# One mixing of three head groups in the first layer, and the output row in two halves: a two-layer decode kernel

## The chip, the cores and the metric

One core of a Trainium2 chip runs the whole kernel. The metric is the device time of one execution in microseconds; the kernel before takes 644.83 us (median of 3 runs, 644.8 to 645.44).

The engines named below: TensorE (PE; its weight loads are listed as PEld), VectorE (DVE), ScalarE (ACT), GpSimd (POOL) and SyncE (SP), which issues the DMA transfers.

## The reference

Four rows of 512 numbers go through two equal layers. Each layer is attention over a long cache (8 key/value heads, each shared by 4 query heads, 8,192 positions of 128 numbers), and then a gated feed-forward block (512 to 1,792 and back). Both layers read the same cache and the same weights.

```python
def reference(A_x, A_k_cache, A_v_cache, A_wq, A_wo, B_x, B_w_gate, B_w_up, B_w_down):
    def _A_ref(x, k_cache, v_cache, wq, wo):
        ...
        q = (lambda x, *d: x.transpose(*d))((x @ wq).reshape(B, Sq, Hq, Dh), 0, 2, 1, 3)
        ...
        scores = jnp.einsum("bhqd,bhkd->bhqk", q, k) * (Dh ** -0.5)
        p = _softmax(scores, axis=-1)
        o = jnp.einsum("bhqk,bhkd->bhqd", p, v)
        return (lambda x, *d: x.transpose(*d))(o, 0, 2, 1, 3).reshape(B, Sq, Hq * Dh) @ wo

    def _B_ref(x, w_gate, w_up, w_down):
        g = _silu(x @ w_gate)
        u = x @ w_up
        return (g * u) @ w_down

    x = A_x
    x = x + _A_ref(_layernorm(x, axis=-1), A_k_cache, A_v_cache, A_wq, A_wo)
    x = x + _B_ref(_layernorm(x, axis=-1), B_w_gate, B_w_up, B_w_down)
    x = x + _A_ref(_layernorm(x, axis=-1), A_k_cache, A_v_cache, A_wq, A_wo)
    x = x + _B_ref(_layernorm(x, axis=-1), B_w_gate, B_w_up, B_w_down)
    return x
```

## The kernel before

**Units and tiles.** The attention of a layer is cut into 16 units `u`, one for each pair of key/value heads `gp` (4 of them, the "groups") and each of the 4 rows `b`. A unit has one K tile and one V tile of 4 MB each. They lie in four large slots of SBUF, used as a ring, and a fifth slot that holds `wq` first. A K tile is handled in eight pieces: VectorE transposes them in place (`turn`, L567, two pieces at a time in most units), and TensorE multiplies each with the queries (`scores`, L593). Then come the row maximum (L599, L604, L607), the exponential on ScalarE (`exps`, L631 to L644), the transpose of the probabilities (`turn_p`, L659), and the products with V (`values`, L731) in four parts. The result is gathered on VectorE (L779, L783), summed over positions (`combine`, L788) and scaled (L793) into `oT`. Work on the V of one unit runs between the score pieces of the next.

**Two lists set the order.** `blocks` holds the score pieces and the parts of V, each with a cost of 0.9 us. `line` holds small steps, each with a gap in microseconds; after every block `advance` takes the block's cost off the first step's gap and emits the steps that have come due. `flush` emits steps without regard to their gaps, all of them if called without a tag. What the lists decide is the order in each engine's instruction stream, once, while the kernel is built; at run time every engine takes its own stream strictly in that order and waits on semaphores.

**Closing a group.** When the four units of a group are done, `close_group` (L825) sees to the output projection of its 8 heads. For all groups but the last of a layer the heads are first *mixed* (`mix`, L806: 16 small products L815 into PSUM and one copy back, L819), which puts them into the order in which `wo` lies in SBUF; then `rows` (L847) multiplies each head's 4 columns with its 512 columns of `wo` (L850), 8 products a group, adding up in one PSUM bank (`OUTB`). After the last but one group, `upright` (L855) turns the 4 x 512 result back to columns in four steps of a ScalarE copy (L864) and a TensorE transpose (L860), and VectorE adds it to `x` (L804). The last group of a layer goes through `out_proj` instead (L875). In the first layer (`L` = 0) groups 0 and 1 are mixed together after group 1, and their rows are emitted by way of the list `later` at the next end of a unit's values; group 2 is mixed alone after unit 11. In the second layer groups 3, 0 and 1 are mixed together after the third of them.

**The hold.** In the first layer the last two pieces of unit 13's K tile (`half_kept`) are kept for the second layer: `finished` (L536) empties `line` with `flush()` and then `hold` (L522) transposes each piece into two PSUM banks, four in all (L533), among them `OUTB` and `LNB`, which the rows and `upright` use. So all rows and turnings stand ahead of the hold in the streams.

**Transfers.** SP issues a transfer as soon as the slot pieces that it overwrites are freed (`freed`, `pump`), in one fixed order. At the end of the first layer the slot of the W weights takes `w_gate`, `w_up` and `w_down`; the later pieces of `w_down` go where `w_gate` lay and are issued as the first products of the feed-forward block (L1016) release it. K tiles of the second layer follow in the same way.

**The output.** The second layer's feed-forward block puts the output together in PSUM bank `STEP`, in four quarters of 128 columns, quarter `j` on rows 32j to 32j+3. `x_rows` (L889) first puts the residual x there: for each pair `c` of quarters four fp32 products with an identity (L893), each of 64 columns; `x_rows(0)` stands in the middle of `center`, `x_rows(1)` ahead of the last products. Then come 14 x 4 products with `w_down` (L1043), and four copies to SBUF, two on VectorE (L1120), two on ScalarE (L1118), and the output's transfer (L1122). `w_down` arrives in three pieces, for 8, 4 and 2 of the 14 steps.

```python
        def quarter(j):
            return bank(STEP)[j * QB:j * QB + B, 0:P]
```

Of the kernel before, what the change touches and what calls it, by code (L numbers as in the profile page):

```python
# [5 lines left out]
ACTF = mybir.ActivationFunctionType  # L6
# [97 lines left out]
def bass_interleave_layers__gqa_block_cached__swiglu_ffn__decode_kernel(  # L104
# [12 lines left out]
    B, _, D = A_x.shape  # L117
# [5 lines left out]
    P = 128  # L123
# [8 lines left out]
    QB = 32  # L132
# [12 lines left out]
    with ExitStack() as es:  # L145
# [132 lines left out]
        def bank(k):  # L278
            return ps[:, k * BANKF:(k + 1) * BANKF]
# [13 lines left out]
            assert o + b <= BANKF  # L293
            return bank(k)[rows, o + a:o + b], f"pb{k}"

        def quarter(j):
            return bank(STEP)[j * QB:j * QB + B, 0:P]

        sem = lambda name: es.enter_context(nc.semaphore(name))
        engines = {"pe": nc.tensor, "act": nc.scalar, "dve": nc.vector, "pool": nc.gpsimd, "sp": nc.sync}  # L300
# [56 lines left out]
        def spot(L, gp):  # L357
            return groups[L].index(gp)
# [466 lines left out]
        def close_group(L, gp, fill):  # L825
            if gp == groups[L][-1]:
                line.extend([[0.5, None, lambda: mix(L, [gp], fill)], [0.7, None, lambda: out_proj(L, gp, fill)]])
                return
            n = spot(L, gp)
            if n < (1, 2)[L]:  # L830
                return
            gs = groups[L][:n + 1] if n == (1, 2)[L] else [gp]
            line.append([0.5, None, lambda: mix(L, gs, fill)])
            turned_back = upright() if gp == groups[L][-2] else []

            def in_rows():
                while gp not in mixed:
                    line.pop(0)[2]()
                for g in gs:
                    rows(L, g)  # L840
                return turned_back
            if turned_back and not L:
                line.extend([[0.7, None, in_rows]] + turned_back)
            else:
                later.append(in_rows)

        def rows(L, gp):  # L847
            for r in range(H2):
                h, o = gp * H2 + r, spot(L, gp) * H2 + r
                T.op("pe", lambda e: e.matmul(bank(OUTB)[0:B, 0:D], lhsT=oT[:, o, :], rhs=wo_sb[:, h, :],  # L850
                                              start=(gp == groups[L][0] and r == 0),
                                              stop=(gp == groups[L][GP - 2] and r == H2 - 1)),
                     reads=[f"wo{gp}", OT[gp]], writes=[f"pb{OUTB}"], sig=(r == H2 - 1))

        def upright():  # L855
            at, name = bank(LNB)[:, 4 * P - XB:4 * P], f"pb{LNB}"

            def step(kt):
                if kt:
                    T.op("pe", lambda e: e.matmul(at[:, (kt - 1) * B:kt * B], lhsT=row, rhs=identf[0:B, 0:B],  # L860
                                                  is_transpose=True, start=True, stop=True),
                         reads=["row", "ident"], writes=[name])
                if kt < KT:
                    T.op("act", lambda e: e.activation(row, bank(OUTB)[0:B, pick2(kt)], ACTF.Copy),  # L864
                         reads=[f"pb{OUTB}"], writes=["row", "pb"])
                else:
                    add_to_x(at, name)
            return [[0.9, None, lambda kt=kt: step(kt)] for kt in range(KT + 1)]
# [19 lines left out]

        def x_rows(c):  # L889
            for e_ in range(2):  # L890
                for m in range(2):
                    kt, o = 2 * c + e_, m * (P // 2)
                    T.op("pe", lambda e: e.matmul(quarter(2 * c + m)[:, e_::2], lhsT=xT[:, kt * B:(kt + 1) * B],  # L893
                                                  rhs=identf[:, o:o + P // 2], start=(e_ == 0), stop=False),
                         reads=["x", "ident"], writes=[f"pb{STEP}"], sig=(e_ == 1 and m == 1))

        def center(between=lambda: None):
            T.op("dve", lambda e: e.tensor_reduce(xs, xT[:].rearrange("p (k b) -> p b k", b=B), AX.X, ALU.add),
# [98 lines left out]
        def ffn(L):  # L997
# [39 lines left out]
            if L == 1:  # L1037
                x_rows(1)
                for i, (a, b) in enumerate(WDS[1]):
                    for fo in range(a, b):  # L1040
                        for j in range(NA):
                            o = s * SL + O_WD + fo * D + j * P
                            T.op("pe", lambda e: e.matmul(quarter(j), lhsT=hT[:, fo * B:(fo + 1) * B],  # L1043
                                                          rhs=kvf[:, o:o + P], start=False, stop=(fo == FO - 1)),
                                 reads=["hT", f"wd{i}"] + rooms[f"wd{i}"], writes=[f"part{j}"],
                                 sig=(fo == b - 1))
                freed(s, DOWN, NB)
                return
# [63 lines left out]
            ffn(L)  # L1112
        assert issued[0] == len(cmds)

        for j in range(NA):
            to = xio[:, j * P:(j + 1) * P]
            if j % 2:
                T.op("act", lambda e: e.activation(to, quarter(j), ACTF.Copy), reads=[f"part{j}"], writes=[f"y{j}"])  # L1118
            else:
                T.op("dve", lambda e: e.tensor_copy(to, quarter(j)), reads=[f"part{j}"], writes=[f"y{j}"])  # L1120
        T.wait_res("sp", reads=[f"y{j}" for j in range(NA)])
        nc.sync.dma_start(out.rearrange("b s d -> (b s) d"), xio).then_inc(sem_out, 16)  # L1122
        nc.sync.wait_ge(sem_out, 16)

# [27 lines left out]
```

## Time and profile before

| | |
|---|---|
| median of 3 runs | 644.83 us |
| the profiled execution | 645.2 us |
| its span, first to last instruction | 642.9 us, 6,981 instructions |
| TensorE matmul busy | 413.0 us (64%), 2,886 instructions |
| TensorE weight loads | 173.2 us (27%), 2,888 instructions |
| VectorE busy | 424.9 us (66%), 597 instructions |
| ScalarE busy | 50.2 us (8%) |
| moved by DMA | 271.76 MB, mean 423 GB/s |
| mean granted clock of TensorE | 0.834 |
| chain that ended last, by share | DMA 60%, VectorE 19%, TensorE 16% |

The span is what the profile's own clock covers; the time of a run also has what lies around it, 2.3 us here. The granted clock is the share of its full clock that TensorE was given. The *chain of waits* follows the work that ended last back from step to step; the *timeline* lists instructions in order of time, with the idle time of the engine before them and who ended it; *windows* give each engine's busy time in a stretch.

### The profile page before, as it was taken

Reading aid. Unit: us, or ns where it says so; the run is one execution under the profiler, and the core shown is the slowest. Engines: PE = TensorE matmul, PEld = TensorE weight load, DVE = VectorE, ACT = ScalarE, POOL = GpSimd, SP = SyncE. Lnnn points to the kernel's source line nnn. Section 1 sums busy time; section 2 is a strip of 40 time slices with the busy share of each in tenths; the row PEclk is TensorE's granted clock in tenths of the full one; section 3 lists DMA queues with packets and bytes.
Section 4 is the critical chain, followed back from the end, with each engine's and each line's share of the span. In section 5 each row is a group of like instructions: output and inputs, shape, how many; then the busy total and the mean of one; then the engine's idle time right before and its main releaser. Section 6 shows DMA issues by size and latency. Waiting matters only on the chain.

```text
span 642.9 us, 6981 instructions
## 1 busy us (share of the span) xinstructions
PE 413.0 (64%) x2886; PEld 173.2 (27%) x2888; DVE 424.9 (66%) x597; ACT 50.2 (8%) x138; POOL 11.9 (2%) x44
## 2 busy tenths in 40 slices
PE   0583476457755757757866977667655477558766
PEld 0231122122222312222325332222222122223224
DVE  5375467456776656776953888977765567656953
ACT  0100000000000000000010300000000000000110
POOL 0000000000000000000000000000000000000000
PEclk9995886688876898768975899998767987679987
DMA  9999999999999999999999999999999999999996
GB/s 365 451 423 414 436 430 432 433 428 423 436 438 427 426 432 433 433 430 429 428 414 386 416 435 431 433 431 429 434 428 430 435 430 432 424 436 429 431 414 261
DMA packets 16014, 271.76 MB, mean 423 GB/s; under 512 B 1640, under 2 KB 1648, under 8 KB 7536
## 3 DMA queue, kind: packets, MB, share of 16 engines
q1 hardware_dynamic: 15984, 271.33, 99.1%
q8 instruction: 22, 0.36, 0.2%
q14 instruction: 8, 0.07, 0.0%
HBM read 271.32 MB, written 0.00 MB: 422 GB/s over the span
## 4 chain that ended last, share of the span: by engine, by line
DMA 60%; DVE 19%; PE 16%; issue 4%; ACT 0%; SPq 0%; POOL 0%; ACTq 0%; DVEq 0%; POOLq 0%
DMA kvf<-in_A_k_cache_dram 45%; DVE kvf L567 14%; DMA kvf<-in_A_v_cache_dram 11%; PE ps L593 10%; DMA kvf<-in_A_wq_dram 3%; PE ps L731 2%; DVE pb L783 2%; DMA kvf<-in_B_w_down_dram 1%; PE ps L982 1%; PE ps L1016 1%; DVE pT L659 1%; DVE pb L779 0%; DVE ps L533 0%; DVE scr L793 0%; PE ps L875 0%
## 5 line engine op out<-in xcount | busy, mean ns | idle before, releaser
L593 PE MATMUL ps<-kvf,zq 128*128 128x512 bf16 x1024 | 291.8, 431 | 185.6 <-DVE kvf L567 178.6
L567 DVE STREAM_TRANSPOSE kvf<-kvf 128x2048 f32<-128x2048 f32 (+1 forms) x133 | 280.5, 2132 | 125.5 <-DMA kvf<-in_A_k_cache_dram 125.3
L593 PEld LDWEIGHTS ps<-kvf,zq 128*128 128x128 bf16 x1024 | 98.9, 108 | 343.1 <-DVE kvf L567 222.6
L731 PE MATMUL ps<-kvf,pT 128*32 128x512 bf16 x960 | 65.8, 396 | 1.4 <-DVE pT L659 1.4
L641 ACT ACTIVATE pb<-ps,tiny 128x512 bf16<-128x512 f32 x32 | 24.9, 777 | 507.8 <-DVE tiny L639 507.8
L659 DVE STREAM_TRANSPOSE pT<-pb 64x512 bf16<-64x512 bf16 x60 | 41.2, 686 | 3.0 <-ACT pb L641 2.0
L783 DVE SCALAR_TENSOR_TENSOR pb<-ps,tiny,pb 128x128 f32<-128x128 f32 x104 | 36.5, 351 | 5.1 <-PE ps L731 1.4
L599 DVE TENSOR_REDUCE tiny<-ps 128x1 f32<-128x512 f32 x32 | 22.0, 688 | 20.5 <-PE ps L593 20.5
L731 PEld LDWEIGHTS ps<-kvf,pT 128*32 128x32 bf16 x960 | 20.8, 98 | 31.1 <-issue 15.4
L788 PEld LDWEIGHTS ps<-sel,pb 128*128 128x128 f32 x64 | 16.5, 266 | 16.4 <-DVE pb L783 8.0
L583 POOL TENSOR_TENSOR zq<-scr,tiny 128x64 bf16<-128x64 bf16 x30 | 9.2, 307 | 525.9 <-PE ps L593 525.9
L607 DVE TENSOR_REDUCE mrm<-ps 1x8 f32<-1x128 f32 x32 | 8.7, 273 | 13.5 <-PE ps L604 13.5
L788 PE MATMUL ps<-sel,pb 128*128 128x8 f32 x64 | 12.1, 262 | 5.4 <-DVE pb L783 5.4
L631 PEld LDWEIGHTS ps<-mrm,tiny 128*128 128x128 f32 x60 | 13.0, 223 | 9.3 <-issue 5.9
L982 PE MATMUL ps<-kvf,xn 128*4 128x512 bf16 x64 | 7.5, 621 | 11.2 <-DMA kvf<-in_A_wq_dram 10.9
L631 PE MATMUL ps<-mrm,tiny 128*128 128x16 f32 x60 | 10.0, 243 | 3.3 <-ACT mrm L644 3.3
L779 DVE TENSOR_SCALAR pb<-ps,tiny 128x128 f32<-128x128 f32 x32 | 10.1, 316 | 2.6 <-PE ps L731 2.6
L850 PE MATMUL ps<-wo_sb,scr 128*4 128x512 bf16 x48 | 10.8, 379 | 0.4 <-DVE scr L819 0.4
L644 ACT ACTIVATE mrm<-head,tiny 128x8 f32<-128x8 f32 x32 | 9.6, 301 | 1.0
L604 PE MATMUL ps<-identf,tiny 128*1 128x128 f32 x32 | 8.6, 270 | 1.2 <-DVE tiny L599 1.2
L804 DVE TENSOR_TENSOR xT<-xT,ps 128x16 f32<-128x16 f32 x6 | 1.0, 172 | 10.6 <-PE ps L860 4.7
L793 DVE TENSOR_TENSOR scr<-ps,rl 128x8 bf16<-128x8 f32 x32 | 5.7, 177 | 3.1 <-PE ps L788 2.1
(88 smaller groups left out, 122.6 us busy)
## 6 DMA issues: line engine op xcount, KB each, us to landing
kvf<-in_A_k_cache_dram SPq DMA_DIRECT2D x27, 4096.0 KB, 31.2
kvf<-in_A_v_cache_dram SPq DMA_DIRECT2D x27, 4096.0 KB, 33.8
kvf<-in_A_v_cache_dram SPq DMA_DIRECT2D x3, 2048.0 KB, 25.0
kvf<-in_A_k_cache_dram SPq DMA_DIRECT2D x11, 512.0 KB, 6.9
kvf<-in_A_k_cache_dram SPq DMA_DIRECT2D x2, 2048.0 KB, 9.4
kvf<-in_A_wq_dram SPq DMA_DIRECT2D x2, 2048.0 KB, 18.1
wo_sb<-in_A_wo_dram SPq DMA_DIRECT2D x4, 1024.0 KB, 41.5
kvf<-in_B_w_gate_dram SPq DMA_DIRECT2D x2, 1792.0 KB, 24.0
```

The costliest lines, as they stand in the source:

```text
L567: T.op("dve", lambda e: e.transpose(w, w), reads=names, writes=names)
L593: T.op("pe", lambda e: e.matmul(bank(bk)[:, 0:SW], lhsT=zq[:, z0:z0 + P], rhs=w[:, :, c // 2, :, c % 2], start=(q == 0 and c == 0), stop=( ...
L599: T.op("dve", lambda e: e.tensor_reduce(mx[:], bank(bk)[:, 0:SW], AX.X, ALU.max), reads=[f"pb{bk}"], writes=["mx"])
L631: T.op("pe", lambda e: e.matmul(at, lhsT=ones, rhs=mrm[:, i * H2:(i + 2) * H2], start=True, stop=True), reads=[f"m8{i}", "rsm", "onesf"], ...
L641: T.op("act", lambda e: e.activation(pb[:], bank(bk)[:, 0:SW], ACTF.Exp, bias=nm, scale=rstd[:, b:b + 1], accum_out=rs), reads=[f"pb{bk}", ...
L659: T.op("dve", lambda e: e.transpose(dst, pb[hp]), reads=["pb", "row"], writes=[name])
L731: T.op("pe", lambda e: e.matmul(bank(k)[j * QB:(j + 1) * QB, q0 * Dh:q1 * Dh], lhsT=p_t[:, t, h, :], rhs=v[:, q0:q1, t, :], start=((last o ...
L779: T.op("dve", lambda e: e.tensor_scalar(into, o, own[:, q:q + 1], None, op0=ALU.mult), reads=[f"pb{k}", "own"], writes=["row"] if last els ...
L783: T.op("dve", lambda e: e.scalar_tensor_tensor(into, o, own[:, q:q + 1], into, op0=ALU.mult, op1=ALU.add), reads=[f"pb{k}", "own", iname], ...
L788: T.op("pe", lambda e: e.matmul(at, lhsT=into, rhs=sel[:], start=True, stop=True), reads=[iname, "sel"], writes=[name])
L850: T.op("pe", lambda e: e.matmul(bank(OUTB)[0:B, 0:D], lhsT=oT[:, o, :], rhs=wo_sb[:, h, :], start=(gp == groups[L][0] and r == 0), stop=(g ...
L982: T.op("pe", lambda e: e.matmul(bank(QK[k])[a * QB:a * QB + B, :], lhsT=xn[:, kt * B:(kt + 1) * B], rhs=wq_sb[:, kt, f:f + W2], start=(kt ...
```

## The change

In the first layer groups 0, 1 and 2 are mixed together after the third of them, with 16 products of 24 columns and one copy of 96 columns a row, instead of two mixings (64 and 32 columns). The rows of the three groups become three steps of `line`, with gaps of 0.7, 1.8 and 1.8 us, followed by the steps of `upright`. The second layer's mixing is as before.

The output is put together in two halves of 256 columns, on rows 0 to 3 and 32 to 35: 14 x 2 products of 256 columns instead of 14 x 4 of 128; two residual products of 128 columns for each half instead of four of 64; one copy of 256 columns on VectorE and one on ScalarE instead of two of 128 on each.

```diff
-        def quarter(j):
-            return bank(STEP)[j * QB:j * QB + B, 0:P]
+        def half_out(j):
+            return bank(STEP)[j * QB:j * QB + B, 0:2 * P]
...
-            n = spot(L, gp)
-            if n < (1, 2)[L]:
+            if gp != groups[L][-2]:
                 return
-            gs = groups[L][:n + 1] if n == (1, 2)[L] else [gp]
+            gs = groups[L][:-1]
             line.append([0.5, None, lambda: mix(L, gs, fill)])
-            turned_back = upright() if gp == groups[L][-2] else []
+            turned_back = upright()
...
-            if turned_back and not L:
-                line.extend([[0.7, None, in_rows]] + turned_back)
+            if L:
+                later.append(in_rows)
             else:
-                later.append(in_rows)
+                line.extend([[0.7 if g == gs[0] else 1.8, None, lambda g=g: rows(L, g)] for g in gs] + turned_back)
...
         def x_rows(c):
             for e_ in range(2):
-                for m in range(2):
-                    kt, o = 2 * c + e_, m * (P // 2)
-                    T.op("pe", lambda e: e.matmul(quarter(2 * c + m)[:, e_::2], lhsT=xT[:, kt * B:(kt + 1) * B],
-                                                  rhs=identf[:, o:o + P // 2], start=(e_ == 0), stop=False),
-                         reads=["x", "ident"], writes=[f"pb{STEP}"], sig=(e_ == 1 and m == 1))
+                kt = 2 * c + e_
+                T.op("pe", lambda e: e.matmul(half_out(c)[:, e_::2], lhsT=xT[:, kt * B:(kt + 1) * B], rhs=identf[:],
+                                              start=(e_ == 0), stop=False),
+                     reads=["x", "ident"], writes=[f"pb{STEP}"], sig=(e_ == 1))
...
-                        for j in range(NA):
-                            o = s * SL + O_WD + fo * D + j * P
-                            T.op("pe", lambda e: e.matmul(quarter(j), lhsT=hT[:, fo * B:(fo + 1) * B],
-                                                          rhs=kvf[:, o:o + P], start=False, stop=(fo == FO - 1)),
+                        for j in range(KT // 2):
+                            o = s * SL + O_WD + fo * D + j * 2 * P
+                            T.op("pe", lambda e: e.matmul(half_out(j), lhsT=hT[:, fo * B:(fo + 1) * B],
+                                                          rhs=kvf[:, o:o + 2 * P], start=False, stop=(fo == FO - 1)),
...
-        for j in range(NA):
-            to = xio[:, j * P:(j + 1) * P]
-            if j % 2:
-                T.op("act", lambda e: e.activation(to, quarter(j), ACTF.Copy), reads=[f"part{j}"], writes=[f"y{j}"])
+        for j in range(KT // 2):
+            to = xio[:, j * 2 * P:(j + 1) * 2 * P]
+            if j:
+                T.op("act", lambda e: e.activation(to, half_out(j), ACTF.Copy), reads=[f"part{j}"], writes=[f"y{j}"])
             else:
-                T.op("dve", lambda e: e.tensor_copy(to, quarter(j)), reads=[f"part{j}"], writes=[f"y{j}"])
+                T.op("dve", lambda e: e.tensor_copy(to, half_out(j)), reads=[f"part{j}"], writes=[f"y{j}"])
```

More of the change, by code (lines that the diff above doesn't have):

```diff
@@ L1113, in bass_interleave_layers__gqa_block_cached__swiglu_ffn__decode_kernel @@
         assert issued[0] == len(cmds)
-        for j in range(NA):
-            to = xio[:, j * P:(j + 1) * P]
-            if j % 2:
-                T.op("act", lambda e: e.activation(to, quarter(j), ACTF.Copy), reads=[f"part{j}"], writes=[f"y{j}"])
-            else:
-                T.op("dve", lambda e: e.tensor_copy(to, quarter(j)), reads=[f"part{j}"], writes=[f"y{j}"])
-        T.wait_res("sp", reads=[f"y{j}" for j in range(NA)])
+        for j in range(KT // 2):
+            to = xio[:, j * 2 * P:(j + 1) * 2 * P]
+            if j:
+                T.op("act", lambda e: e.activation(to, half_out(j), ACTF.Copy), reads=[f"part{j}"], writes=[f"y{j}"])
+            else:
+                T.op("dve", lambda e: e.tensor_copy(to, half_out(j)), reads=[f"part{j}"], writes=[f"y{j}"])
+        T.wait_res("sp", reads=[f"y{j}" for j in range(KT // 2)])
         nc.sync.dma_start(out.rearrange("b s d -> (b s) d"), xio).then_inc(sem_out, 16)
```

## The prediction, made before the changed kernel ran

> **What bounds the kernel now.** I read the page's summary first, then the chain of waits for the places where it leaves DMA, then the timeline there, and last the busy times by window around the end of the first layer. The page:
>
> ```profile
> DMA  9999999999999999999999999999999999999996
> ```
>
> The DMA engines are busy all the time: 271 MB at 423 GB/s fill the span up to the last 16 us. So work saved on an engine gains nothing unless it starts a transfer that the DMA engines lack, and added work costs only if they run dry or if it lies behind the last transfer. The two halves of the change lie near the only two such places. The first-layer half, timeline of the 14th unit (u=13):
>
> ```profile
> 290.25 1.89 PE L850 MATMUL ps<-wo_sb,scr 128*4 128x512 bf16 x8 [0.40 <-DVE scr L819]
> ...
> 294.48 0.17 DVE L804 TENSOR_TENSOR xT<-xT,ps 128x16 f32<-128x16 f32 x1 [4.38 <-PE ps L860]
> 294.56 2.38 DVE L533 STREAM_TRANSPOSE ps<-kvf 128x1024 f32<-128x1024 f32 x2
> ...
> 298.07 2.29 DVE L567 STREAM_TRANSPOSE kvf<-kvf 128x2048 f32<-128x2048 f32 x1
> ```
>
> (Start, duration, engine, line, shapes; in brackets the idle time before and who ended it.) Eight row products, then the four turnings back (L864, L860), then VectorE, which has stood still 4.38 us, goes on with the hold (L533) and the next K tile. From there to the end of the layer:
>
> ```profile
> 336.95 1.58 DVE L783 SCALAR_TENSOR_TENSOR pb<-ps,tiny,pb 128x128 f32<-128x128 f32 x4 [0.57 <-PE ps L731]
> ...
> 343.31 1.61 SPq L93 DMA_DIRECT2D kvf<-in_B_w_down_dram  x3
> ```
>
> The one place in these 40 us where VectorE waits because a transfer is late is the 0.57 us ahead of 336.95 (TensorE got its V tile at 336.06). The issue at 343.31 waits for the first products of the feed-forward block, thus for all of this. Windows (us, then busy us and counts of PE, PEld, DVE, ACT, POOL, then granted clock, DMA share, GB/s):
>
> ```profile
> 340.00:342.00 2.00, 1.28 (x34) 1.23 (x34) 0.45 (x3) 0.00 (x0) 0.00 (x0) 0.50 1.02 410
> ...
> 343.00:344.00 1.00, 1.00 (x27) 1.00 (x25) 0.01 (x1) 0.00 (x0) 0.00 (x0) 0.50 0.90 339
> 344.00:345.00 1.00, 1.00 (x36) 1.00 (x36) 0.03 (x1) 0.56 (x2) 0.00 (x0) 0.50 0.90 281
> ```
>
> Here the rate falls from 410 to 281 GB/s: some DMA engines already have nothing to do until that issue reaches them. The other place is the tail:
>
> ```profile
> 637.69 0.59 PE L893 MATMUL ps<-identf,xT 128*4 128x64 f32 x8
> ...
> 638.19 1.34 PE L1043 MATMUL ps<-kvf,pb 128*4 128x128 bf16 x44
> ...
> 640.17 0.49 PE L1043 MATMUL ps<-kvf,pb 128*4 128x128 bf16 x12 [0.64 <-issue]
> 640.69 0.60 DVE L1120 CAST pb<-ps 4x128 bf16<-4x128 f32 x2 [2.55 <-PE ps L1043]
> 640.72 0.56 ACT L1118 ACTIVATE pb<-ps 4x128 bf16<-4x128 f32 x2 [3.92 <-PE ps L1043]
> 641.36 0.29 SPq L1122 DMA_DIRECT2D out_dram<-pb  x1
> ```
>
> and the window of it:
>
> ```profile
> 637.40:640.80 3.40, 2.62 (x78) 1.79 (x75) 0.71 (x4) 0.08 (x1) 0.00 (x0) 0.50 0.18 68
> ```
>
> Everything here is on the path. TensorE's granted clock is 0.50, and it stands still 0.64 us after 44 of the 56 products, waiting for nothing the profile names ("issue").
>
> **The first mixing.** Removed: one mixing of two groups (16 products L815, one copy L819) at 210 us, and 16 row products L850 in 3.62 us at 214.5. Nothing is gained there: the timeline shows VectorE idle 5.24 us for a K transfer at 199.78, and again 5.25 us at 277.64, so whatever is saved in between is waited out; I set it to 0. Added: the one mixing at 288.45 takes 24 columns a product instead of 8 (the second layer's same form takes 0.42 us, as now: 0), its copy 96 columns instead of 32 (first layer's 64 columns 0.22 us, 32 columns 0.19: +0.06), and 24 row products where 8 stood. The order of the built kernel shows all 24 in a row on TensorE, between the same two sets of scores: the hold empties the list of due work before it. The second layer already has that form:
>
> ```profile
> 585.38 5.34 PE L850 MATMUL ps<-wo_sb,scr 128*4 128x512 bf16 x24
> ```
>
> 5.34 - 1.89 = 3.45 us, with the copy 3.5. Queued behind: on TensorE the turnings back and the last scores, on VectorE (in order) the add L804, the hold and every later K transpose, and SP's releases. No transfer is late at first: the page gives 31 us from issue to landing for a 4 MB K load, of which the transfer itself takes 4.19 MB / 0.43 = 9.8 us, so about 20 us lie in the queue ahead of each. But the delay has nowhere to go: VectorE is busy 3.89 of 4.00 us in 299 to 303 and 3.00 of 3.00 in 303 to 306, the next K tile follows at once, and then VectorE's chain of maximum, transposes and gathers runs on without a late transfer until 336. There 0.57 us are taken up: 2.9 us remain, and the issue of 343.31 comes at 346.2.
>
> What does that cost the DMA engines? The two transfers before it (256 KB each, issued at 338.42 and 338.80, 8.4 and 8.7 us to landing) are the last work they have; the slowest engine ends it at 338.80 + 8.7 = 347.5, the faster ones by 344 to 345, as 339 and 281 GB/s of 410 show. The issue of 343.31 (256 KB, 0.6 us of transfer) landed 4.9 us later, behind the rest of that queue; the rate is back about 2 us after the issue, which I take as the latency. So the new issue brings data at about 348: the slowest engine then loses 348 - 347.5 = 0.5 us, a fast one the whole 2.9. Bounds 0.4 and 2.9. Since all engines start level again at 348, and a transfer has landed when its last engine has, I lean to the fast ones' loss: 2.2. In between, the feed-forward block's waits for w_up (0.56 us) and w_down (0.91 and 0.68) absorb most of what TensorE is late, so later issues come under 1 us late and cost nothing more. From 370 us on the DMA engines move 424 to 436 GB/s in every slice but the last two, so 2.2 us stay to the end. **+2.2 us.**
>
> **The output.** 28 products of 256 columns replace 56 of 128. Now four products with different output rows run side by side: 44 in 1.34 us are 11 steps, (1.34 - 0.31) / 10 = 0.103 us a step, 0.31 being one product's own duration. (L893 shows two side by side.) With two halves a step has two products of twice the columns: 0.21 us. 14 steps: 13 x 0.21 + 0.42 = 3.2 us, where 14 steps now take 1.34 + 3 x 0.103 = 1.65. The rows of x ahead of it: eight records two by two in 0.59 us now; in halves, four records of 128 columns one after the other, about 4 x 0.21 = 0.85. The products of the other half could start beside them, so their start moves by 0 to 0.3 us; I take 0.3. The first set (0.32 us in the chain of waits, at 633.85, clock still 1.00) grows by some 0.2, of which the wait of L1016 for xn hides half: +0.1, or 0.2 without that cover.
>
> The stall of 0.64 us: TensorE's code comes in 22 transfers of 16 KB on its own queue (one at 637.57), one for every 266 of its 5,849 records. The stall ends two and a half us after that transfer, in the middle of products that have no wait of their own, so I read it as late code. The change takes 32 records of the mixing, 16 of x rows and 56 of products out of TensorE's stream, 104 in all; the 24 that stood behind the stall then belong to the block before it, and the stall goes. Its cover, the wait for the last w_down piece, is over before the slower products need it.
>
> Last product's end: 638.19 + 0.1 + 0.3 + 3.2 = 641.8 instead of 640.17 + 0.49 = 640.66: +1.1. Copies: two in a row on each engine (0.56 us on ScalarE) become one of 256 columns; ScalarE's 128 columns take 0.27 and 512 (L641) 0.78, so 0.44: -0.1. **+1.0 us**, between -0.8 (the new step also takes 0.1 us, and the stall is gone: the last product ends near 640.0) and +1.7 (the stall stays).
>
> By the Trainium skill, "TensorE: Matmul & The Clock Gate", Part 1, a window of 3.4 us that is busy lifts the clock to full for the next. The trace agrees: TensorE is busy 3.00 of 3.00 us in 303 to 306 at clock 0.50, and has 0.95 in 306 to 310. The longer stream would fill the window 637.4 to 640.8 and halve the steps behind it; by that rule the sum is 0.2 us less. That needs windows at the same phase, so I leave the sum.
>
> **Sum.** 2.2 + 1.0 = +3.2 us. The profiled execution took 645.2 us, 2.3 us around its span of 642.9; it is 0.37 above the median of 644.83, inside the spread of the three runs (644.8 to 645.44). I add to the median: 648.0 us, span 646.1.
>
> **Rivals.** 0.2% is 1.3 us, about what these runs tell from no change.
> - *The delay never reaches the DMA queue* (not slower). Place: 294 to 336 us; it decides if 2.5 of the 3.5 us are caught up, for then the issue of 343.31 reaches the slower engines in time. For it: in 299 to 306 TensorE runs at clock 0.50 to 0.57, and fuller windows may keep it at 1.00. Against: VectorE is full there and its transposes don't follow that clock. Time 644.83 + 1.0 = 645.8, no change by the bound.
> - *The products don't cost by column*: the clock is full in the tail, or the step stays near 0.1 us. Then -0.8 with 2.2: 646.2, still slower. Against: the windows 634 to 637.4 and 637.4 to 640.8 show 0.51 and 0.50.
> - *The stall stays*: 648.0 + 0.64 = 648.6. The Trainium skill, "Runtime: NRT & Kernel Launch", Instruction fetch mechanics, says that crossing a code block is mostly hidden; by that rule the stall has another cause and remains. The row shows 0.64 us and no other releaser.
> - *The DMA engines lose the whole 2.9*: 648.7, inside my range.
> That the change isn't carried out can be left out: the built order shows it.
>
> **Chances.** Forecast 0.64 (own range 647.2 to 648.7), delay absorbed 0.14, products cheap 0.09, stall stays 0.10, something faster that I don't see 0.03. Slower: 0.64 + 0.09 + 0.10 = 0.83; same 0.14; faster 0.03. The range 645.7 to 649.2 reaches from the absorbed case to whole loss and stall together, short of its extreme.
>
> **What would show it.** Right: 24 row products at about 290 in 5.3 us; the hold near 298; the issue of 343.31 near 346; a window about 344 to 348 with GB/s far below 281; the 28 products in one stretch of about 3.2 us, no 0.64 us gap, copies of about 0.4 us. Wrong: transpose of the next K tile still at 298, or the three w_down issues still at 343 (first half); products in under 2 us (second half).

## The result and the profile after

The changed kernel takes 648.95 us (median of 6 runs, 647.94 to 650.01) against 645.35 us for the kernel before on the same chip (6 runs): a ratio of 1.0058, 95% interval 1.0047 to 1.007. On a second chip it was 648.46 against 645.07 (5 and 21 runs), 1.0044 (1.0031 to 1.0056). So the change costs 2.8 to 3.7 us by the two ratios (2.0 to 4.5 by their intervals); 3.2 had been forecast, and all eleven runs lie between 647.56 and 650.01.

The time of a run is the span and the rest that lies around it, and the change moves the two in opposite directions. On the second chip the median span is 646.6 us against 642.8, 3.8 more; the rest is 1.8 us against 2.3, 0.5 less. The forecast took the rest as unchanged.

The profile shown is of the execution of 650.01 us (span 648.2), the slowest of the eleven. Where that matters, the profile of the second chip (647.98 us, span 646.2) stands beside it.

The end of the first layer, timeline (start, duration, engine, line, shapes; in brackets the idle time before and who ended it):

```profile
290.06 5.34 PE L849 MATMUL ps<-wo_sb,scr 128*4 128x512 bf16 x24 [0.67 <-DVE scr L819]
...
297.75 0.17 DVE L804 TENSOR_TENSOR xT<-xT,ps 128x16 f32<-128x16 f32 x1 [7.83 <-PE ps L859]
297.83 2.38 DVE L533 STREAM_TRANSPOSE ps<-kvf 128x1024 f32<-128x1024 f32 x2
301.69 2.29 DVE L567 STREAM_TRANSPOSE kvf<-kvf 128x2048 f32<-128x2048 f32 x1
...
345.72 1.55 SPq L93 DMA_DIRECT2D kvf<-in_B_w_down_dram  x3
...
351.19 0.59 PE L1051 MATMUL ps<-pb,kvf 128*128 128x4 bf16 x16 [1.05 <-DMA kvf<-in_B_w_down_dram]
352.62 0.59 PE L1051 MATMUL ps<-pb,kvf 128*128 128x4 bf16 x16 [0.84 <-DMA kvf<-in_B_w_down_dram]
```

The 24 row products take 5.34 us where 8 took 1.89; the idle time of VectorE ahead of the add (L804) grows from 4.38 to 7.83 us; the hold and the next K tile come 3.3 and 3.6 us later, and the issue of the three `w_down` pieces comes at 345.72 instead of 343.31. The waits of the feed-forward block for `w_down`, 0.91 and 0.68 us before, have grown, not vanished. The windows there (us, then busy us and counts of PE, PEld, DVE, ACT, POOL, granted clock, DMA share, GB/s):

```profile
343.00:344.00 1.00, 0.66 (x25) 0.57 (x22) 0.27 (x2) 0.00 (x0) 0.00 (x0) 0.50 0.90 350
344.00:345.00 1.00, 0.59 (x2) 0.50 (x2) 0.32 (x3) 0.00 (x0) 0.00 (x0) 0.50 0.61 236
345.00:346.00 1.00, 0.91 (x29) 0.94 (x29) 0.38 (x3) 0.00 (x0) 0.00 (x0) 0.50 0.28 96
346.00:347.00 1.00, 1.00 (x27) 1.00 (x25) 0.00 (x0) 0.44 (x2) 0.00 (x0) 0.50 0.40 59
347.00:348.00 1.00, 1.00 (x39) 1.00 (x37) 0.52 (x3) 0.37 (x2) 0.00 (x0) 0.50 0.96 291
```

The rows from 345 to 347 us are the hole: 96 and 59 GB/s where the kernel before never fell below 281. The tail:

```profile
642.22 0.80 PE L891 MATMUL ps<-identf,xT 128*4 128x128 f32 x3
642.72 0.37 PE L1041 MATMUL ps<-kvf,pb 128*4 128x256 bf16 x1
...
642.89 3.30 PE L1041 MATMUL ps<-kvf,pb 128*4 128x256 bf16 x27
646.06 0.41 DVE L1118 CAST pb<-ps 4x256 bf16<-4x256 f32 x1 [3.39 <-PE ps L1041]
646.23 0.37 ACT L1116 ACTIVATE pb<-ps 4x256 bf16<-4x256 f32 x1 [4.89 <-PE ps L1041]
646.67 0.29 SPq L1120 DMA_DIRECT2D out_dram<-pb  x1
```

The 28 products run in one stretch and there is no "issue" gap. From the start of the second x rows to the end of the products it is 642.89 + 3.30 - 642.22 = 3.97 us; before, 640.66 - 637.69 = 2.97 with the stall in it. The output's transfer leaves 0.48 us after the last product instead of 0.70.

### The profile page after: what moved, and what is told of

The parts are those of the page before. It is cut to its first block, busy times and chain, and to the rows that moved or that the text cites. A ratio compares the mean times of both kernels' runs of the same rounds, so it can differ in the third digit from the quotient of the medians.

```text
span 648.2 us, 6874 instructions
## 1 busy us (share of the span) xinstructions
PE 414.5 (64%) x2834; PEld 173.5 (27%) x2836; DVE 424.4 (65%) x595; ACT 50.0 (8%) x137; POOL 11.8 (2%) x44
## 4 chain that ended last, share of the span: by engine, by line
DMA 51%; DVE 26%; PE 17%; issue 4%; ACT 1%; SPq 0%; POOL 0%; POOLq 0%; DVEq 0%; ACTq 0%
DMA kvf<-in_A_k_cache_dram 47%; DVE kvf L567 19%; PE ps L593 8%; PE ps L731 3%; DMA kvf<-in_A_wq_dram 3%; DVE pb L783 3%; DVE pT L659 1%; DMA kvf<-in_B_w_down_dram 1%; PE ps L980 1%; DVE pb L779 1%; PE ps L849 1%; PE ps L1014 1%; PE ps L1041 0%; DVE scr L793 0%; PE ps L788 0%
## 5 line engine op out<-in xcount | busy, mean ns | idle before, releaser
L804 DVE TENSOR_TENSOR xT<-xT,ps 128x16 f32<-128x16 f32 x6 | 1.0, 172 | 15.8 <-PE ps L859 9.7
L940 DVE STREAM_TRANSPOSE ps<-ps 128x512 f32<-128x512 f32 x4 | 2.9, 721 | 7.3 <-PE ps L980 7.2
```

## The experiments

Twelve sets of runs followed, of ten kernels, one of them twice, and of the changed kernel again. They came in three groups, each on one chip beside runs of the kernel before (645.5, 645.07 and 645.41 us). The first four take the change apart and imitate its delay. The table has the times and what the first layer's end shows in each kernel's one profile. "Span" and "rest" are medians of the runs; "moved" is the sum of two windows, 340 to 346 and 346 to 352 us, GB/s times 6 us each.

| kernel | median, us | ratio to before (95%) | span, us | rest, us | add L804 at | `w_down` issue at | moved, 340 to 352, MB |
|---|---|---|---|---|---|---|---|
| before | 645.35 | 1 | 642.8 to 643.3 | 2.2 to 2.3 | 294.48 | 343.31 | 4.58 |
| changed | 648.95 | 1.0058 (1.0047 to 1.007) | 647.1 | 1.8 | 297.75 | 345.72 | 3.47 |
| changed, second chip | 648.46 | 1.0044 (1.0031 to 1.0056) | 646.6 | 1.8 | 297.72 | 345.32 | 3.66 |
| mixing alone | 647.02 | 1.0023 (1.0013 to 1.0032) | 644.85 | 2.2 | 298.00 | 346.09 | 3.65 |
| output alone | 645.48 | 1.0001 (0.999 to 1.0012) | 643.65 | 1.8 | 294.36 | 343.32 | 4.43 |
| output alone, second chip | 646.33 | 1.0015 (1.0006 to 1.0024) | 644.5 | 1.8 | 294.19 | 343.70 | 4.16 |
| before + 16 row products, late | 647.36 | 1.0028 (1.0017 to 1.0038) | 644.7 | 2.95 | 297.03 | 344.86 | 3.99 |
| before + 8 row products, late | 644.73 | 0.9991 (0.9982 to 1.0) | 642.9 | 1.9 | 295.11 | 343.13 | 4.60 |
| before + 16 row products, early | 646.29 | 1.0009 (0.9999 to 1.0018) | 643.25 | 3.1 | 294.12 | 343.64 | 4.44 |
| before, early rows cut short | 645.34 | 1.0003 (0.9994 to 1.0012) | 643.1 | 2.3 | 294.28 | 342.96 | 4.57 |
| changed, rows cut short | 646.39 | 1.0018 (1.0009 to 1.0027) | 644.6 | 1.8 | 294.88 | 343.08 | 4.34 |

The spans of the kernel before are 643.3, 642.8 and 643.2 us beside the three groups; for its six runs beside the changed kernel's first six the record has none. Two cautions go with the table. The rest differs from kernel to kernel by up to 0.9 us, and no run shows what sets it, so small differences in time are better read from the spans. And one profile scatters: in eight profiles of kernels without added work at 290 us (before, the output alone twice, 16 row products early, early rows cut short, and the three kernels with tiny products further down) the issue lies between 342.96 and 343.70 us, "moved" between 4.16 and 4.58 MB, and the last add L804 of the kernel between 632.70 and 634.07 us. The late issues (344.86 to 346.09) and the holes (3.47 to 3.99 MB) are clear of that scatter, the smallest hole, 3.99, by little; their sizes are known to some 1 us only.

### The two halves alone

The mixing alone: the diff above without its output part.

```diff
-            if n < (1, 2)[L]:
+            if gp != groups[L][-2]:
                 return
...
```

> The first mixing alone (first-layer half of the change, quarters as before). Theory of the delay (24 row products ahead of the hold, 3.5 us, of which the end of the layer absorbs 0.57): the three w_down issues near 346 instead of 343.3, a hole in the DMA rate at 344 to 348, and 2.2 to 2.9 us more, 647.5 to 648.3 us. Rival, the delay is absorbed: 645.3 us, issues at 343. The code-block theory adds: 32 records of TensorE fewer take the last products into the block before, so their 0.64 us stall is gone though the products are the same 56; where the stall is something else it stays.

Measured: +1.5 us, below the expected 2.2 to 2.9. The issue comes at 346.09 and the hole is there. And the stall in the tail is gone, as the count of records asks: the mixing takes 32 of them out of TensorE's stream ahead of it. Timeline of the tail:

```profile
639.89 0.60 PE L892 MATMUL ps<-identf,xT 128*4 128x64 f32 x8
640.39 1.93 PE L1042 MATMUL ps<-kvf,pb 128*4 128x128 bf16 x56
643.01 0.29 SPq L1121 DMA_DIRECT2D out_dram<-pb  x1
```

All 56 products of 128 columns run in one stretch. From the last add L804 (635.24) to the output's transfer it is 7.77 us here and 8.33 in the kernel before. So the 1.5 us is the mixing's price less the 0.56 us that the tail gives back.

The output alone: the diff without its mixing part.

```diff
-                        for j in range(NA):
-                            o = s * SL + O_WD + fo * D + j * P
+                        for j in range(KT // 2):
+                            o = s * SL + O_WD + fo * D + j * 2 * P
...
```

> The output in halves alone (mixing as before). Theory that the products cost by column: 14 steps in 3.2 us instead of 1.65, no stall, copies 0.1 to 0.2 us shorter: 0.8 to 1.0 us more, 646.2 us. Rival, steps as long as before: 0.8 us less, 644.6 us. The first layer's issue stays at 343.3.

Measured: level with before in the first ten runs. The transfer of the output left at 642.10, 0.74 us later than before, so the tail had the forecast's direction but not its size. It ran again, beside the changed kernel, on another chip:

> The output in halves with the mixing as before, again, since its first ten runs were level with the kernel before while its tail ended 0.74 us later. Theory (the prediction's +1.0 less what the clock gave back in its tail): 0.5 to 1.0 us above before, 645.9 to 646.5. Rival (products in halves cost nothing in all, because the longer stream lifts the clock as often as not and the stall is gone): within 0.3 us of before.

> The changed kernel once more, beside its output half alone on the same chip, to see what the two halves add up to. Theory: the first mixing costs 2.2 to 2.9 us at the end of the first layer, the halves cost 1.75 us (products 3.3 against 1.65, x rows +0.4, copies -0.2, from the tails seen so far), and the 0.64 us stall is gone once, not twice: 3.3 to 4.0 us above the kernel before, 648.8 to 649.5, and 2.9 to 3.5 above the output half alone if that one costs 0.5 to 1.0. Rival: the two parts add up plainly, 1.5 (mixing alone) and 0 (output alone), and what was above that in the first six runs was the chip: 647.0.

Measured: +1.3 us by the medians (ratio 1.0015), within what was expected. The changed kernel is 3.4 us above the kernel before, as expected, so the rival's 647.0 is out; but it is only 2.13 us above this kernel (648.46 - 646.33), less than the 2.9 to 3.5 expected.

The two profiles of the output half differ by 1.2 us of span (643.7 and 644.9). Of that, 0.94 us is there before the tail, at the last add L804 (633.13 and 634.07), where this edit changes nothing. Behind it the tails differ by 0.24 us, and what stands out in them is the products. The first one:

```profile
638.87 2.75 PE L1042 MATMUL ps<-kvf,pb 128*4 128x256 bf16 x27
```

and the second:

```profile
639.47 3.34 PE L1042 MATMUL ps<-kvf,pb 128*4 128x256 bf16 x27
```

The windows of the first (columns as above):

```profile
637.40:640.80 3.40, 3.40 (x57) 3.08 (x56) 1.07 (x4) 0.00 (x0) 0.00 (x0) 0.50 0.20 75
640.80:642.00 1.20, 0.82 (x12) 0.50 (x8) 0.41 (x1) 0.34 (x1) 0.00 (x0) 0.96 0.00 0
```

and of the second:

```profile
637.40:640.80 3.40, 3.40 (x74) 3.11 (x73) 1.56 (x6) 0.25 (x1) 0.00 (x0) 0.50 0.32 121
640.80:642.00 1.20, 1.20 (x15) 1.10 (x13) 0.00 (x0) 0.00 (x0) 0.00 (x0) 0.50 0.00 0
```

In one execution the granted clock rises to 0.96 at 640.8 and the last steps run at twice the pace; in the other it stays at 0.50 until the products are over. Same kernel, 0.59 us apart; the first x rows, at a lower clock in the first one, give 0.29 of it back. The prediction had named this (0.2 us less, "windows at the same phase") and left it out of the sum; its own figures, with the last product ending at 641.8, leave 1.0 us behind 640.8, and half of that is 0.5, not 0.2. The Trainium skill, "TensorE: Matmul & The Clock Gate", Part 1, calls the window free-running and the point of the lift different from run to run; these two executions agree.

### The delay alone

Row products that feed nothing, put ahead of group 2's rows (late) or of those of groups 0 and 1 (early) in the kernel before.

```diff
+                if not L and gp == 2:
+                    idle_rows(16)
                 for g in gs:
                     rows(L, g)
```

> The kernel before with 16 extra row products into an unused bank, ahead of group 2's rows in the first layer (added work, output unchanged). They need no copy first, so they start 0.4 us sooner than rows: delay 3.05 us. Theory: it costs like the mixing alone less some 0.4, 2.0 to 2.5 us more, 647.5 us. If the cost of the change came from the mixing itself or from the row steps' order, and not from TensorE time in this place, nothing: 645.3 us.

The early one has `gp == 1` in the condition.

> The kernel before with the same 16 extra row products, but ahead of group 1's rows near 214 us in the first layer (added work, output unchanged). Theory: they are waited out there, 0 us, 645.3 us. If added TensorE time costs wherever it stands (by its clock or its share): as much as in the late place, 647.5 us.

Measured by the medians: late +1.9 us, just under what was expected, and early +0.8, with a ratio whose interval touches no change. The spans part the two more clearly: late +1.4 us (644.7 against 643.3), early nothing (643.25); the rest around the span is 0.7 and 0.9 us more. Of the 2.55 us by which the late one shifts the add L804, 1.55 reach the `w_down` issue; the hole is 4.58 - 3.99 = 0.59 MB, at the mean rate of 0.42 MB a us 1.4 us. So time spent by TensorE at 290 us is dear and the same time at 214 us is free in the span; the mixing's own form (24 columns, one copy) is not needed for the loss. Half of the dose, 8 products:

> The kernel before with 8 more row products of 512 columns ahead of group 2's rows (about 1.8 us), half of the delay tried before; they feed nothing. The stall moves behind the 36th product and stays. Theory (fast DMA engines run dry at once, 0.57 us of the delay is taken up at 336): w_down issue about 1.2 us later, 344.5, and 0.6 to 1.2 us above before. Rival (DMA engines run dry only once the issue is later than some 345, because the slowest still have work): within 0.3 us of before. Third (the whole delay counts): +1.8.

Measured: not slower, and nothing of the delay is left at the issue (343.13). Part of the 8 products ran in the idle time ahead of the copy L819. The add stands 0.63 us later than in the kernel before, and this profile had been 0.43 us early ahead of the products (the K transpose at 285.82 instead of 286.25), so they put in 1.06 us, not 1.8. Following VectorE's instructions one by one against the kernel before, this profile is 0.63 us late to 304, 0.45 from 306 to 330, and 0.2 early from 333. The V products show why, half dose, timeline:

```profile
331.93 0.61 PE L731 MATMUL ps<-kvf,pT 128*32 128x512 bf16 x8
332.37 1.04 PE L731 MATMUL ps<-kvf 128*32 128x512 bf16 x16
...
335.87 0.35 PE L731 MATMUL ps<-kvf 128*32 128x384 bf16 x4 [1.33 <-DMA kvf<-in_A_v_cache_dram]
```

and the kernel before:

```profile
331.71 1.04 PE L731 MATMUL ps<-kvf,pT 128*32 128x512 bf16 x8
332.54 1.60 PE L731 MATMUL ps<-kvf 128*32 128x512 bf16 x16
```

The same products are faster, at a granted clock of 1.00 in 332 to 334 us instead of 0.58, and then both kernels wait for the same V tile. The mixing alone shows what that tile's waits take up by themselves: it is 3.53 us late at the add, 3.46 up to 336, and 2.79 at the issue, the steps being 0.47 at the first part of the tile and 0.20 at the second. So a lateness of about 0.7 us disappeared there in that profile, and 0.45 would have. The theory's 0.6 to 1.2 us fell because the products delayed the add by 1.06 us instead of 1.8 and the rest was waited out ahead of the issue; the rival named the right time for the wrong reason, since the issue was not late at all.

### The row products, taken away in both places

In both kernels 15 of the row products of groups 0 and 1 in the first layer are cut to 4 of their 512 columns.

```diff
-                T.op("pe", lambda e: e.matmul(bank(OUTB)[0:B, 0:D], lhsT=oT[:, o, :], rhs=wo_sb[:, h, :],
+                w = B if not L and gp != 2 and (gp or r) else D
+                T.op("pe", lambda e: e.matmul(bank(OUTB)[0:B, 0:w], lhsT=oT[:, o, :], rhs=wo_sb[:, h, 0:w],
```

> The changed kernel with 15 of its 24 row products of the first layer cut to 4 of their 512 columns, so that most of the projection of head groups 0 and 1 is left out of the first layer; every instruction stays in its place and the record counts stay. Theory that the mixing's whole price is the time of the added row products: the 24 take about 2.4 us instead of 5.3, the w_down issue comes back to about 343.5 to 343.9, and the run takes what the output half alone takes, 0 to 1.0 us above before: 645.1 to 646.3, 2.3 to 3.0 below the changed kernel. Rival (the price comes from the mixing of 24 columns, its copy or the missing early work): stays near 648.5.

> The kernel before with 15 of the 16 row products at 214.5 us cut to 4 of their 512 columns, so that most of the projection of head groups 0 and 1 is left out of the first layer; record counts stay, so the stall in the tail stays behind the 44th product. Theory of the prediction (work removed there is waited out before 277.6): within 0.5 us of before, 645.1. Rival (the early rows lie on the path, as the 0.8 us of the early delay hinted): faster by 0.8 to 3.2 us.

Measured in the changed kernel: +1.0 us by the medians (646.39 to 645.41) instead of the whole change's 2.8 to 3.7; just above the theory's range, between the two results of the output half alone, and far from the rival's 648.5. Timeline:

```profile
290.05 2.48 PE L850 MATMUL ps<-wo_sb,scr 128*4 128x512 bf16 x24 [0.66 <-DVE scr L819]
...
294.88 0.17 DVE L804 TENSOR_TENSOR xT<-xT,ps 128x16 f32<-128x16 f32 x1 [4.97 <-PE ps L860]
```

The mixing of 24 columns, its copy and the missing early work are all still there; with the row products short, the add is back within 0.4 us and the issue at 343.08. So the price of the mixing is the time of the added row products. In the kernel before, the early rows take 0.73 us instead of 3.62 and the run takes the same time (645.34 to 645.41): work removed at 214 us is worth nothing, as the forecast had it.

### The stall in the tail

Tiny products that feed nothing, put at the very start, where TensorE waits for its first data; they shift every later instruction in TensorE's stream by two records each.

```diff
+        for _ in range(8):
+            T.op("pe", lambda e: e.matmul(bank(TOT)[0:QB, 0:B], lhsT=ident[:, 0:QB], rhs=ident[:, 0:B], start=True, stop=True),
+                 reads=["ident"], writes=[f"pb{TOT}"], sig=False)
```

> The kernel before with 8 tiny products (16 records) at its start, where TensorE waits for its first data; they feed nothing. Theory that the stall in the tail is late TensorE code at a fixed count of records: the stall moves 8 products earlier, from behind the 44th to behind the 36th, and stays about 0.6 to 0.9 us. Rival (the stall belongs to the place, a wait that the profile does not show): it stays behind the 44th product.

Timeline with 8 of them:

```profile
638.21 1.13 PE L1043 MATMUL ps<-kvf,pb 128*4 128x128 bf16 x36
640.40 0.70 PE L1043 MATMUL ps<-kvf,pb 128*4 128x128 bf16 x20 [1.06 <-issue]
```

(one run, 645.21 us), and with the 16 early row products of the delay:

```profile
638.93 0.92 PE L1050 MATMUL ps<-kvf,pb 128*4 128x128 bf16 x28
640.12 0.92 PE L1050 MATMUL ps<-kvf,pb 128*4 128x128 bf16 x28 [0.28 <-issue]
```

The stall stood behind the 44th product; 8 products more at the other end of the kernel put it behind the 36th, 16 more behind the 28th. So its place is a count in the stream, not a piece of the work. The trace's last 16 KB code transfer starts at 637.57 (before), 637.85 and 637.78 us, and TensorE goes on 2.60, 2.55 and 2.34 us later.

How long the stall lasts is not fixed. With 8 row products more, late, it stands behind the 36th product, as expected, and lasts 0.48 us. With the early rows cut short, where the count is that of the kernel before, the expected gap behind the 44th product isn't there: the products wait for `w_down` first, and only the weight loads stand still, for 0.21 us. With the 16 row products late the border lies behind the 28th product, as with the early ones, and there is no gap at all:

```profile
640.66 1.66 PE L1050 MATMUL ps<-kvf,pb 128*4 128x128 bf16 x56
```

There the code transfer starts at 638.87, 1.79 us ahead of the products; in the kernel before it is 0.62 us ahead. That fits code that has arrived by the time the products need it.

With 110 or 170 tiny products the border lies elsewhere:

> The kernel before with 170 tiny products (340 records) at its start, where TensorE waits for its first data; they feed nothing. Theory of late code at a fixed count of records: the last code block now begins some 60 products of other work ahead of the tail's products, at a place where TensorE waits for data anyway; the 56 products run in one stretch of about 1.65 us, the last ends near 640.0 instead of 640.66, and the run takes 0.6 us less than the kernel before: about 644.9. Rival (the stall belongs to the place): the gap stays behind the 44th product and the time is the same. Third: the added block costs a fetch more and shifts others, time up by 0 to 0.5.

> The kernel before with 110 tiny products (220 records) at its start, where TensorE waits for its first data; they feed nothing. The tail then holds one block border only, 246 records ahead of the end, in the gate and up products, and none in the last 112. Theory: the 56 products run in one stretch of 1.65 us with no gap at all (170 tiny products left one of 0.20 us), the last ends near 639.85, and the run takes 0.6 to 0.8 us less than before. Rival: the fetch for the block comes too late there as well, and the gap of 0.5 us or more shows among the gate and up products: same time as before.

170, timeline:

```profile
638.25 0.27 PE L1043 MATMUL ps<-kvf,pb 128*4 128x128 bf16 x2
638.73 1.66 PE L1043 MATMUL ps<-kvf,pb 128*4 128x128 bf16 x54 [0.20 <-issue]
```

110, timeline with the weight loads:

```profile
638.85 2.05 PE L1043 MATMUL ps<-kvf,pb 128*4 128x128 bf16 x56
639.89 0.31 PEld L1043 LDWEIGHTS ps<-kvf,pb 128*4 128x4 bf16 x16 [0.30 <-DMA kvf<-in_B_w_down_dram]
```

The gap shrinks to 0.20 us with 170 (now behind the second product, 108 records ahead of the end) and is gone with 110. But with 110 the products meet the wait for the last `w_down` pieces, and the last one ends at 640.91, not at the expected 639.85. The times are 644.7 against 645.07 (ratio 0.9992, 0.9983 to 1.0001) and 644.85 against 645.41 (0.9993, 0.9984 to 1.0002): 0.4 to 0.6 us less by the medians, with intervals that just reach no change. Most of that lies around the span: the spans are 642.8 against 642.8 and 643.0 against 643.2 us, the rest 1.8 against 2.3 and 2.2. That either beats the kernel before is therefore not shown; that the stall moves is.

## Why the prediction was right, step by step

**The sum.** 3.2 us were forecast, and 3.4 and 3.6 came by the medians. That they lie so close is in part luck: on the second chip the change costs 3.8 us in the span and saves 0.5 us around it, a term that the sum doesn't have.

**What bounds it.** Right: work at 214 us free in both directions (0.9994 to 1.0012 when cut, the span unchanged when added), the same work at 290 us paid.

**Row products and delay (3.5, then 2.9 at the issue).** 5.34 us, and the add 3.24 to 3.53 us later: right (3.5 in all three profiles, counted from each one's own K transpose at 286 us). "There 0.57 us are taken up": 0.67 with the mixing alone, at the place named, and the issue 2.8 us late. In the other two profiles it was 0.9 and 1.2 us (issue 2.4 and 2.0 us late), in part because the V products at 331 to 336 us ran at a higher clock than in the kernel before. The first rival had named fuller clock windows, at 299 to 306, and 0.2 us was gained there; but the output half alone, which has no delay, gains as much there, at a granted clock of 1.00 in 303 to 306 us instead of 0.50, so that is a difference of the clock between executions. The rival as a whole, 2.5 of 3.5 us caught up, is out: the hole is in all three profiles.

**What the DMA engines lose (2.2 of 2.9).** The holes, at 0.42 MB a us: (4.58 - 3.47) / 0.42 = 2.6 us, 2.2 on the second chip, 2.2 with the mixing alone, against issues 2.4, 2.0 and 2.8 us late. By these, about all of the lateness is lost, as one rival had it and more than the share I took; that the lateness itself was under 2.9 made up for it, by luck. Against the output half alone on the second chip (4.16 MB) the hole is 1.2 us only, so the share itself is not settled. In run time the mixing costs 2.13 us (changed less output alone, one chip) or 1.5 plus the tail's 0.56 (mixing alone): 2.1 both ways, where 2.2 stood. That feed-forward waits "absorb most of what TensorE is late" held for the mixing alone (2.8 us late at the issue, 0.8 at 352 us) and not for the changed kernel (2.4 and 1.8; on the second chip 2.0 and 1.1). The wait for `w_up`, 0.56 us before, is gone in all three, but the waits for `w_down` were 1.05 and 0.84 us in one profile of the changed kernel and 0.67 and 0.86 in the other, since the pieces they wait for are the ones issued late. It cost little: in 352 to 372 us the DMA engines moved 406 to 410 GB/s in these profiles, against 413 before.

**The products (1.65 to 3.2 us).** 3.30 to 3.34 at clock 0.50, in one stretch: right, and the rival that they don't cost by column is out, save for the last steps in an execution whose clock rises in time (2.75).

**The x rows (+0.3 and +0.1).** From the start of the second x rows to the end of the products 3.97 us, 1.0 more than before, as summed. The first x rows move L1016 by 0.1 to 0.4 us: from 0.43 us (633.78 to 634.21) to 0.82 in the first profile of the output half, 0.53 in the second and in the first chip's profile of the changed kernel.

**The copies (-0.1).** 0.48 us from the last product to the transfer instead of 0.70: -0.2.

**The stall (0.64, gone).** Right that it goes, and shown that its place moves with the count of records. That the count alone takes it away in the changed kernel isn't shown, since the products there also come later and run slower, and late products had no stall in the late delay either. Taking it away was worth less than its length: 0 to 0.2 us of span with 170 and 110 tiny products, with 110 for the reason that the forecast had set aside, the wait for `w_down`. The Trainium skill, "Runtime: NRT & Kernel Launch", Instruction fetch mechanics, describes code that arrives in blocks of 256 instructions and calls the crossing mostly hidden. The blocks agree with the place of the stall: 24 records ahead of the end before, 108 with 340 records more, and 24 + 340 - 108 = 256. "Mostly hidden" does not hold in every profile: 0.64 us idle in the kernel before, 1.06 with 8 tiny products, none with the late delay.

**The output's +1.0.** From the last add L804 to the output's transfer it is 8.33 us before, 8.98 and 9.22 with the output alone, 9.12 with the rows cut short and 9.21 in the changed kernel: 0.65 to 0.89 more, a little under the forecast, and part of the scatter is the clock as shown. (In the second chip's profile of the changed kernel it is 9.87, with 0.43 us of waiting for `w_gate`.) In run time the output half shows 0.0, +1.3 and, with the rows cut short, +1.0, and each has 0.4 to 0.5 us less around the span; the spans are 0.35, 1.7 and 1.4 us longer.

**What stays open.** The mixing's 2.1 and the tail's 0.65 to 0.89 make about 2.9 us of span; 3.8 were measured. Why the output half's span grew by more than its tail on the second and third chips, and by less on the first, no run shows. Part of the difference may be one more effect of the clock. The two profiles of the changed kernel differ by 2.0 us of span. In the longer one VectorE is 0.6 us later at 585 us, 1.6 us after a K tile that lands later (591.94 and 593.50), and 3.3 us after this stretch of the second layer, timeline of the longer one:

```profile
608.32 1.75 PE L593 MATMUL ps<-kvf,zq 128*128 128x512 bf16 x4 [0.90 <-POOL zq L583]
...
610.20 1.85 PE L593 MATMUL ps<-kvf,zq 128*128 128x512 bf16 x4
...
612.24 0.17 DVE L804 TENSOR_TENSOR xT<-xT,ps 128x16 f32<-128x16 f32 x1 [1.86 <-PE ps L859]
```

and of the other:

```profile
606.58 1.03 PE L593 MATMUL ps<-kvf,zq 128*128 128x512 bf16 x4 [0.90 <-POOL zq L583]
...
607.69 1.04 PE L593 MATMUL ps<-kvf,zq 128*128 128x512 bf16 x4
...
608.92 0.17 DVE L804 TENSOR_TENSOR xT<-xT,ps 128x16 f32<-128x16 f32 x1 [0.28 <-PE ps L859]
```

Four score products take 1.75 and 1.85 us where they take 1.03 and 1.04, at a granted clock of 0.57 in 608 to 612 us against 1.00, and VectorE's add waits 1.86 us for them. That this part of the program meets a low clock more often in the changed kernel than before would need many profiles of both; it wasn't tried. So what the change costs, 2.8 to 3.7 us, is settled better than the share of it that the clock has.

## What to carry to other kernels

Before costing a moved step, look for the next place where its engine, or one that depends on it, waits for a transfer: 16 row products were free in the span at 214 us and cost 1.4 to 2.1 us at 290, and 8 cost nothing even there, since idle time ahead of them and the next wait for a transfer took them up. Measure a transfer hole in bytes over a window that holds the whole of it, and take the same window of several profiles without the hole, which scattered here by 0.42 MB, 1 us; the hole then has a price with a width. Look at the span and at what lies around it apart: here the rest moved by 0.5 to 0.9 us and no run shows why. And where a short, dense stretch of instructions ends a kernel, its time also hangs on where code blocks and the rise of the clock fall, so that an edit far away can shift it by half a microsecond.

## What the runs showed of the hardware that was not expected

- TensorE stood still for up to 1.06 us in the middle of products that wait for nothing. The place moved one product for each product added ahead (from behind the 44th to behind the 36th and the 28th); TensorE went on 2.3 to 2.6 us after the start of a 16 KB code transfer (2.60, 2.55, 2.34, and 2.60 with 170 tiny products). Where the products came 1.79 us after that start instead of 0.62, there was no stall.
- The same 27 products took 2.75 and 3.34 us in two executions of one kernel: in the first the granted clock rose from 0.50 to 0.96 at 640.8 us, in the second it did not.
- The time around the span, 2.2 to 2.3 us for the kernel before, was 1.8 to 1.9 with the output in halves, with tiny products or with 8 row products more, and 2.95 and 3.1 with 16 row products more. What sets it stays open.
